# A new hand-written sequence for the operations of a fused attention and swish MLP kernel, and a longer planned transfer for the spread of the reciprocals

## The chip, the cores and the metric

One core of one Trainium2 chip runs the whole kernel. The metric is the device time of one execution in microseconds, lower is better; a time in the tables is the median of several runs. Beside it stands the profile of one execution, whose span runs from the first instruction to the last.

## The reference

Attention over batch 4, 8 heads, 768 positions, head size 64. Three heads (0, 2 and 6) are causal over all positions; the other five are streaming heads, which keep the causal window of 64 positions and the first 4 positions. The result goes through an MLP with a swish whose slope differs per column.

```python
scores = q @ k.T / sqrt(64)
mask   = causal                        for retrieval heads (0, 2, 6)
mask   = causal & (pos_k < 4 | pos_q - pos_k < 64)   for the others
a = softmax(where(mask, scores, -1e9)) ; x = a @ v     # x: 3072 x 512
h = x @ w_in                                           # 512 x 2048
out = (h * sigmoid(beta * h)) @ w_out                  # 2048 x 512, float32
```

## The kernel before

The work is cut into 8 units: unit n = 2b + u is batch b and half u (384 positions, `NQ`). Per unit:

- **Attention.** q, k and v are loaded in float32 on SP's DMA queue, cast to bf16 (tile `c` for q and k, `vb` for v) and turned. Units 0 to 2 turn q and k with TensorE (`T`) and copy the result out (`QK`). From unit 3 on, three loads per tensor fill a `wf` buffer (`load_block`, line 380), GpSimd casts it in six pieces (`cast_block`, line 389), and three DMA transposes on SP write `QK` (`turn_block`, line 397; op `QKb`). Scores `S` go to PSUM, ScalarE takes the exponential (`E`), VectorE multiplies by 0/1 masks (`masks`, line 684, op `M`: a tensor_tensor with both inputs in SBUF). `sums_d` (line 747) adds the columns on TensorE, `pv` (line 840, op `o`) multiplies with v.
- **The window's other operands.** `shift_v` (line 421, op `vs`) copies v shifted by 64 rows, on VectorE or GpSimd; `sink_v` (line 432, op `vk`) makes three small copies on VectorE; `load_edge` and `cast_edge` (`vef`, `ve`) fetch a few rows of v; `kp_copy` (line 556, op `KP`, nine copies) packs keys.
- **The reciprocals, from unit 2 on.** `sums_copy` puts the sums into SBUF, `sums_turn` lays them out by DMA, `recips_d` inverts them, `spread_w` writes them to DRAM (`rd`), and `spread_r` (line 793) reads every row back into 64 partitions (`R`). VectorE's `norm` (line 887, op `xT`) multiplies `o` by `R`. So four steps stand on SP's queue between the sums and `xT`.
- **MLP.** Per unit 16 steps `h` (`mm1`, four matmuls each), ScalarE's tanh (`t`), VectorE's scalar_tensor_tensor (`g`, one SBUF and one PSUM input), and 48 matmuls `m` (`mm2`) in pieces of three; the outputs are copied (`ob`) and stored.
- **Weights.** Eight loads of 1 MB (`wf`,i,0 to 3 for w_in and `wf`,o,0 to 3 for w_out), each cast by GpSimd in four pieces (`wi`,0 to 15 and `wo`,0 to 15). Loads of weights, of v and of the q and k blocks share three `wf` buffers (`RINGS`, line 217): a load is not issued before all casts of an earlier one have run.

**What sets the order.** Every operation is registered with `add` (line 129) with its engine or choice of engines, a planned cost, what it needs and gives, and the buffers that it takes and drops. `_Plan.run` (line 137) goes through the 1096 operations in the order of the list `SEQUENCE` (line 37), takes the engine of each free choice from the string `CHOICE`, gives each a planned start, and the program is written out sorted by it. Each engine's queue, SP's DMA queue too, is then executed strictly in that order: an instruction that waits holds everything behind it on its engine. The planned cost and `dma` of an operation have no other effect than on these starts, and on the number of filling matmuls that keep TensorE busy in unit 0 (`fill`, line 513).

All profile lines carry line 112, the helper that records every operation, so groups are told apart by their tiles. The core of the planner:

```python
e = {"a": "act", "d": "dve", "g": "pool"}[choice[i]] if i in choice else list(costs)[0]
t = max([now[e]] + [done[n][0] - (0.2 if e == "pe" and done[n][1] == e else 0.0) for n in needs])
...
order.append((t, i, f, e, t - was))
...
return [x[2:] for x in sorted(order, key=lambda x: x[:2])]
```

Of the kernel before, what the change touches and what calls it, by code (L numbers as in the profile page):

```python
# [34 lines left out]


SEQUENCE = [
    474, 475, 0, 2, 468, 10, 8, 6, 4, 469, 473, 14, 466, 477, 463, 471, 12, 81, 1, 478, 77, 25, 3, 16, 26, 9,
    33, 11, 479, 20, 35, 34, 5, 27, 18, 36, 28, 7, 29, 42, 31, 30, 13, 53, 480, 32, 82, 15, 50, 41, 37, 51,
    464, 38, 54, 52, 44, 17, 45, 47, 39, 48, 85, 23, 46, 24, 79, 40, 49, 78, 56, 89, 21, 104, 55, 57, 490, 19,  # L40
    43, 58, 59, 22, 100, 60, 61, 101, 482, 62, 83, 476, 80, 91, 73, 63, 90, 485, 102, 74, 75, 484, 64, 103,
    76, 116, 465, 117, 65, 118, 66, 86, 67, 69, 119, 120, 491, 87, 68, 492, 122, 70, 71, 481, 123, 72, 483,
    121, 470, 125, 494, 520, 500, 84, 493, 126, 106, 524, 107, 105, 521, 93, 528, 525, 489, 532, 526, 486, 95,
    128, 127, 529, 112, 92, 88, 522, 97, 536, 530, 113, 495, 114, 537, 108, 115, 109, 124, 129, 538, 503, 540,
    501, 110, 541, 547, 111, 488, 542, 487, 548, 131, 134, 94, 132, 551, 505, 130, 135, 549, 137, 98, 138,
    139, 502, 555, 533, 133, 142, 140, 136, 504, 534, 559, 552, 141, 143, 510, 563, 96, 553, 556, 560, 144,
    99, 467, 561, 496, 155, 557, 499, 564, 145, 497, 157, 498, 156, 506, 515, 523, 146, 507, 570, 509, 527,
    565, 508, 571, 169, 147, 158, 531, 572, 161, 148, 149, 535, 511, 163, 150, 512, 151, 167, 153, 152, 574,
    513, 165, 514, 154, 578, 575, 159, 582, 173, 576, 579, 171, 586, 580, 583, 518, 218, 584, 517, 587, 516,
    588, 519, 592, 596, 593, 539, 597, 168, 543, 546, 170, 544, 550, 164, 598, 222, 188, 160, 554, 594, 189,  # L50
    162, 558, 166, 172, 184, 562, 185, 174, 186, 600, 187, 190, 193, 181, 191, 566, 196, 569, 192, 573, 175,
    194, 604, 220, 567, 198, 605, 219, 577, 601, 201, 221, 581, 199, 197, 585, 602, 225, 589, 200, 228, 608,
    590, 195, 606, 224, 203, 609, 612, 223, 204, 227, 610, 619, 202, 206, 613, 205, 623, 226, 620, 207, 614,
    176, 627, 621, 208, 177, 591, 628, 568, 631, 178, 624, 209, 629, 179, 210, 635, 625, 632, 545, 636, 633,
    229, 237, 637, 642, 239, 646, 238, 235, 650, 182, 643, 240, 647, 644, 595, 241, 211, 648, 654, 212, 242,
    472, 269, 599, 651, 249, 655, 652, 658, 236, 250, 656, 232, 603, 286, 252, 183, 607, 659, 254, 230, 660,
    213, 611, 257, 243, 251, 615, 255, 231, 180, 618, 622, 616, 273, 256, 626, 253, 244, 630, 245, 634, 247,
    246, 638, 258, 248, 641, 639, 645, 287, 233, 259, 617, 214, 260, 216, 215, 261, 649, 272, 653, 217, 271,
    280, 657, 234, 664, 276, 668, 288, 665, 661, 279, 669, 666, 275, 672, 662, 270, 676, 278, 670, 673, 262,
    680, 274, 677, 674, 684, 678, 277, 681, 691, 685, 682, 281, 695, 263, 686, 692, 699, 326, 283, 696, 693,  # L60
    703, 697, 700, 707, 704, 701, 714, 663, 705, 708, 718, 289, 715, 709, 722, 716, 290, 726, 264, 293, 667,
    719, 291, 671, 720, 675, 727, 329, 723, 730, 728, 315, 282, 724, 679, 731, 292, 328, 295, 732, 683, 284,
    298, 687, 296, 690, 294, 694, 319, 297, 300, 688, 698, 301, 285, 702, 303, 299, 265, 302, 304, 267, 327,
    689, 266, 305, 330, 268, 706, 306, 710, 307, 713, 711, 717, 370, 736, 317, 740, 721, 741, 321, 725, 737,
    318, 324, 729, 738, 322, 742, 733, 331, 316, 744, 325, 734, 748, 320, 745, 308, 752, 749, 746, 323, 756,
    750, 753, 763, 757, 754, 309, 767, 366, 758, 764, 771, 768, 765, 775, 769, 772, 779, 712, 773, 332, 786,
    780, 790, 776, 781, 334, 310, 777, 787, 739, 336, 788, 794, 335, 798, 791, 368, 377, 337, 795, 743, 369,
    339, 796, 747, 792, 338, 373, 802, 799, 346, 803, 800, 751, 349, 640, 804, 755, 333, 347, 350, 759, 367,
    762, 760, 341, 371, 766, 344, 340, 770, 374, 372, 342, 774, 345, 348, 351, 375, 778, 343, 354, 782, 376,
    352, 355, 313, 783, 353, 311, 378, 383, 356, 312, 785, 784, 357, 314, 789, 358, 793, 808, 812, 412, 816,  # L70
    813, 387, 817, 814, 797, 390, 386, 801, 388, 820, 818, 359, 392, 389, 821, 360, 805, 809, 416, 822, 395,
    824, 810, 391, 393, 828, 415, 806, 835, 829, 394, 839, 414, 836, 830, 397, 837, 361, 825, 843, 840, 826,
    847, 841, 844, 851, 845, 858, 396, 384, 811, 418, 815, 848, 379, 421, 398, 819, 849, 413, 859, 860, 852,
    862, 807, 853, 866, 863, 399, 870, 400, 419, 864, 867, 823, 871, 422, 874, 872, 364, 401, 417, 868, 875,
    362, 876, 420, 385, 402, 380, 363, 827, 735, 403, 365, 831, 404, 834, 832, 838, 423, 381, 842, 846, 429,
    880, 382, 833, 884, 881, 888, 885, 850, 886, 431, 882, 889, 854, 405, 432, 890, 857, 406, 861, 433, 426,
    865, 425, 855, 869, 424, 856, 430, 761, 873, 427, 434, 436, 892, 407, 877, 435, 896, 878, 893, 900, 897,
    894, 879, 907, 898, 901, 911, 908, 902, 915, 909, 912, 919, 916, 913, 923, 917, 920, 930, 924, 921, 934,
    925, 938, 935, 942, 931, 410, 932, 936, 408, 939, 883, 943, 409, 887, 411, 946, 891, 940, 443, 947, 952,
    446, 948, 895, 944, 444, 956, 953, 960, 954, 899, 445, 961, 447, 438, 962, 903, 439, 437, 906, 964, 441,  # L80
    440, 910, 904, 957, 448, 442, 905, 914, 428, 449, 918, 451, 922, 965, 452, 450, 926, 958, 453, 927, 966,
    929, 928, 454, 933, 455, 968, 972, 969, 979, 970, 937, 980, 983, 981, 941, 984, 945, 973, 985, 987, 974,
    456, 991, 988, 457, 995, 992, 989, 949, 993, 996, 955, 997, 1002, 950, 1006, 1003, 959, 1007, 1004, 458,
    1010, 1008, 1014, 1011, 1018, 1015, 1012, 963, 1016, 1019, 951, 967, 1020, 971, 975, 978, 976, 982, 977,
    986, 990, 994, 998, 1001, 999, 1005, 459, 461, 460, 1009, 462, 1013, 1017, 1021, 1024, 1022, 1028, 1025,
    1023, 1032, 1000, 1029, 1026, 1036, 1030, 1033, 1040, 1037, 1034, 1044, 1038, 1041, 1051, 1045, 1042,
    1055, 1046, 1052, 1059, 1056, 1053, 1063, 1057, 1060, 1067, 1064, 1061, 1073, 1065, 1068, 1076, 1027,
    1077, 1069, 1031, 1074, 1078, 1079, 1075, 1082, 1080, 1085, 1083, 1081, 1035, 1084, 1086, 1039, 1087,
    1043, 1047, 1050, 1048, 1054, 1049, 1058, 1062, 1066, 1070, 1088, 1071, 1089, 1072, 1092, 1090, 1091,
    1093, 1094, 1095,  # L90
]
CHOICE = (
    "dggdaaadgddddaddaddagddaaagaaaggddggddaadaddddaggadaaddggddggaggadddadgaddaaadddaaadaadddddaadaaa"
)


# [21 lines left out]
class _Plan:  # L118
# [10 lines left out]
    def add(self, eng, cost, f, needs=(), gives=(), take=(), drop=(), dma=0.0, mode=None, port=False, begun=()):  # L129

        needs = dict.fromkeys(m for n in needs for m in self.same.get(n, [n]))
        one = isinstance(eng, str)
        alts = [(eng, cost)] if one else list(zip(eng, cost))
        self.ops.append((0, len(self.ops), dict(alts), (lambda e: f()) if one else f, tuple(needs), tuple(gives),
                         tuple(take), tuple(drop), dma, mode, port, tuple(begun)))
# [53 lines left out]
def kernel(  # L189
# [14 lines left out]
    pe, dve, act, pool, sp = (_Ordered(tc, e) for e in (nc.tensor, nc.vector, nc.scalar, nc.gpsimd, nc.sync))  # L204
# [3 lines left out]
    NP = len(PAIRS)  # L208
# [4 lines left out]
    def tpool(name, bufs, space=None):  # L213
# [6 lines left out]
        sp=2, b=4, **{f"es{pi}_{u}": 1 for pi in range(NP) for u in range(2)})  # L220
# [741 lines left out]
    add = plan.add  # L962
    ENG = {"act": act, "dve": dve, "pool": pool, "sp": sp}

    def attention(n, early):
        x = units[n]
        b, u = x.b, x.u

        for pi in range(NP if n < TD else 0):
            for nm in ("q2", "k2"):  # L970
                e = "act" if n == 0 and nm == "k2" else "sp"
                add(e, 0.47, lambda pi=pi, nm=nm, e=e: load_qk(x, pi, nm, ENG[e]), dma=0.63,
                    gives=[("f", n, pi, nm)], take=[(nm + "f", (n, pi), 1)])
# [127 lines left out]
        else:  # L1101
# [3 lines left out]
                take=[("rec", n, 1)], drop=[("sc", n)])  # L1105
            add("dve", 0.35, lambda: recips_d(x), needs=[("sum_t", n)], gives=[("rec", n)])
            add("sp", 0.4, lambda: spread_w(x), needs=[("rec", n)], gives=[("rd", n)], dma=0.1, drop=[("rec", n)])
            add("sp", [1.33, 2.65][u], lambda: spread_r(x), needs=[("rd", n)], gives=[("R", n, t) for t in range(NP)], dma=[4.1, 4.4][u],
                take=[("R", n, 2)] + ([("q2f", (n, "x"), 1)] if u else []))
        for g in range(2):  # L1110
            drop = [(f"es{pi}_{u}", n) for pi in [(0, 1), (2, 3)][g]] + [("vb", b), ("vs", n), ("VE", b)] + ([("KP1", "k")] if n == 1 else [])
# [129 lines left out]
```

The softmax here doesn't subtract the row's maximum and nothing guards it: scores larger than these inputs give would overflow.

## Time and profile before

| | |
|---|---|
| median of 13 runs | 244.98 us (242.68 to 246.46) |
| the profiled execution's own time | 244.87 us |
| its span | 243.2 us |
| time outside the span | 1.67 us |
| TensorE busy | 223.8 us, 92% of the span |
| VectorE, ScalarE, GpSimd busy | 158.4, 137.7, 87.1 us |
| mean granted TensorE clock | 0.993 |
| moved by DMA | 43.14 MB, mean 177 GB/s |
| HBM read, written | 32.38 MB, 6.37 MB |

A group's row gives busy time, mean duration and the idle time of its engine before it, with what ended most of that idle time. A row of the timeline begins with the start in us from the span's start and the duration; "x" is the number of instructions merged; in brackets stands the idle time before it and its releaser. "SPq" is SP's DMA queue. The DMA share of a stretch can exceed 1 where packets of several transfers overlap.

### The profile page before, as it was taken

Reading aid. Unit: us, or ns where it says so; the run is one execution under the profiler, and the core shown is the slowest. Engines: PE = TensorE matmul, PEld = TensorE weight load, DVE = VectorE, ACT = ScalarE, POOL = GpSimd, SP = SyncE. Lnnn points to the kernel's source line nnn. Section 1 sums busy time; section 2 is a strip of 40 time slices with the busy share of each in tenths; the row PEclk is TensorE's granted clock in tenths of the full one; section 3 lists DMA queues with packets and bytes.
Section 4 is the critical chain, followed back from the end, with each engine's and each line's share of the span. In section 5 each row is a group of like instructions: output and inputs, shape, how many; then the busy total and the mean of one; then the engine's idle time right before and its main releaser. Section 6 shows DMA issues by size and latency. Waiting matters only on the chain.

```text
span 243.2 us, 6062 instructions
## 1 busy us (share of the span) xinstructions
PE 223.8 (92%) x2362; PEld 127.9 (53%) x2388; DVE 158.4 (65%) x359; ACT 137.7 (57%) x231; POOL 87.1 (36%) x201
## 2 busy tenths in 40 slices
PE   7795789989979999899999989999999999999994
PEld 6562355545545455446554545564465455465553
DVE  4795599954797869569575457787566847436620
ACT  3656667254859706572379638744674745208611
POOL 6203849497591957263817300624200000000000
PEclk9999799999999999999999999999999999999999
DMA  6999799999978997999999999999620110702012
GB/s 206 254 267 316 234 228 337 310 318 202 189 186 192 213 185 176 170 262 189 233 197 254 210 164 178 211 174 239 199 67 0 46 45 13 214 3 86 0 43 86
DMA packets 92108, 43.14 MB, mean 177 GB/s; under 512 B 75936, under 2 KB 84848, under 8 KB 92080
## 3 DMA queue, kind: packets, MB, share of 16 engines
q1 hardware_dynamic: 90992, 41.98, 75.6%
q10 hardware_dynamic: 1088, 0.79, 1.0%
q8 instruction: 18, 0.29, 0.5%
q14 instruction: 10, 0.08, 0.1%
HBM read 32.38 MB, written 6.37 MB: 159 GB/s over the span
## 4 chain that ended last, share of the span: by engine, by line
PE 63%; DMA 16%; POOL 6%; SPq 5%; issue 4%; DVE 3%; ACT 2%; ACTq 0%; POOLq 0%
PE b L112 55%; PE sp L112 7%; SPq L112 5%; DMA k2f<-in_k_dram 5%; DMA wf<-in_moe_w_in_dram 3%; DMA QK<-c 3%; DMA vf<-in_v_dram 3%; POOL c L112 2%; DMA wf<-in_v_dram 2%; POOL vs L112 1%; DVE gT L112 1%; POOL vb L112 1%; POOL w_in L112 1%; POOL VE L112 1%; ACT t L112 1%
## 5 line engine op out<-in xcount | busy, mean ns | idle before, releaser
L112 ACT ACTIVATE t<-b,beta_h 128x384 f32<-128x384 f32 x128 | 72.2, 582 | 49.0 <-PE b L112 36.5
L112 DVE SCALAR_TENSOR_TENSOR gT<-t,b 128x384 bf16<-128x384 f32 x128 | 68.9, 551 | 40.9 <-ACT t L112 37.4
L112 PE MATMUL b<-xT,w_in 128*128 128x384 bf16 x512 | 92.6, 330 | 2.8 <-DVE mask_s L112 1.1
L112 PE MATMUL b<-w_out,gT 128*128 128x512 bf16 (+1 forms) x374 | 87.6, 370 | 2.5 <-issue 1.6
L112 PEld LDWEIGHTS <-w_in 128*128 128x128 bf16 x512 | 49.3, 99 | 40.1 <-issue 3.6
L112 PEld LDWEIGHTS <-gT 128*128 128x128 bf16 x400 | 37.0, 98 | 38.5 <-issue 2.2
L112 ACT ACTIVATE es<-sp 128x768 bf16<-128x768 f32 (+2 forms) x64 | 48.6, 805 | 11.6 <-PE sp L112 11.4
L112 POOL CAST c<-wf 128x256 bf16<-128x256 f32 x60 | 23.3, 433 | 26.0 <-DMA wf<-in_q_dram 16.2
L112 PE MATMUL sp<-QK 64*64 64x64 bf16 (+6 forms) x402 | 18.8, 234 | 4.5 <-DMA QK<-c 1.7
L112 ACT ACTIVATE osb<-b 128x512 f32<-128x512 f32 (+1 forms) x13 | 7.4, 566 | 22.5 <-PE b L112 18.9
L112 PEld LDWEIGHTS <-QK 64*64 64x64 bf16 (+1 forms) x402 | 10.1, 105 | 15.2 <-issue 11.6
L112 POOL CAST vb<-wf 128x512 bf16<-128x512 f32 x18 | 11.5, 654 | 14.4 <-DMA wf<-in_v_dram 14.4
L112 POOL COPY KP<-QK 128x64 bf16<-128x64 bf16 (+5 forms) x38 | 10.3, 318 | 16.2 <-DMA QK<-c 14.5
L112 DVE TENSOR_TENSOR xT<-sp,R 128x768 bf16<-128x768 f32 (+3 forms) x18 | 11.6, 684 | 7.0 <-PE sp L112 5.8
L112 DVE TENSOR_TENSOR es<-es,mask_c 128x256 bf16<-128x256 bf16 (+2 forms) x32 | 13.4, 427 | 3.2 <-ACT es L112 3.1
L112 POOL CAST w_in<-wf 128x512 bf16<-128x512 f32 x16 | 9.7, 650 | 15.7 <-DMA wf<-in_moe_w_in_dram 15.7
L112 DVE TENSOR_TENSOR es<-es,mask_s 128x800 bf16<-128x800 bf16 (+5 forms) x24 | 13.1, 555 | 2.5 <-ACT es L112 2.5
L112 PE MATMUL sp<-es,vb 128*64 128x64 bf16 (+3 forms) x243 | 13.7, 237 | 0.0
L112 DVE COPY vs<-vb 64x1536 bf16<-64x1536 bf16 (+4 forms) x19 | 11.0, 593 | 3.0 <-POOL vb L112 2.7
L112 PEld LDWEIGHTS <-vb 128*64 128x64 bf16 x243 | 11.5, 111 | 0.5
L112 POOL COPY vs<-vb 64x1536 bf16<-64x1536 bf16 (+2 forms) x7 | 9.6, 1374 | 4.2 <-issue 4.0
L112 POOL CAST w_out<-wf 128x512 bf16<-128x512 f32 x16 | 10.1, 673 | 2.5 <-DMA wf<-in_moe_w_out_dram 2.2
(91 smaller groups left out, 167.5 us busy)
## 6 DMA issues: line engine op xcount, KB each, us to landing
out_dram<-osb SPq DMA_DIRECT2D x23, 256.0 KB
wf<-in_v_dram SPq DMA_DIRECT2D x18, 256.0 KB
wf<-in_moe_w_out_dram SPq DMA_DIRECT2D x4, 1024.0 KB
wf<-in_q_dram SPq DMA_DIRECT2D x15, 256.0 KB
wf<-in_k_dram SPq DMA_DIRECT2D x15, 256.0 KB
R<-rd SPq DMA_DIRECT2D x9, 384.0 KB
wf<-in_moe_w_in_dram SPq DMA_DIRECT2D x4, 768.0 KB
q2f<-in_q_dram SPq DMA_DIRECT2D x12, 192.0 KB
```

Of the source, the lines that this page charges most:

```text
L112: ins = f(*a, **k)
```

## The change

Three things are edited: the list `SEQUENCE`, the string `CHOICE` and two planned durations.

```diff
 SEQUENCE = [
-    474, 475, 0, 2, 468, 10, 8, 6, 4, 469, 473, 14, 466, 477, 463, 471, 12, 81, 1, 478, 77, 25, 3, 16, 26, 9,
...
+    474, 475, 6, 466, 4, 8, 14, 468, 12, 478, 467, 20, 10, 0, 2, 16, 5, 469, 473, 9, 7, 33, 471, 29, 77, 34,
...
 CHOICE = (
-    "dggdaaadgddddaddaddagddaaagaaaggddggddaadaddddaggadaaddggddggaggadddadgaddaaadddaaadaadddddaadaaa"
+    "aaddagaggdgdadadadaadddaddaaddgaagggdaaadaadaaaddaaaddaggdgdgaggadggdgdaadaadaaadaadadadadddadaaa"
 )
...
-            add("sp", [1.33, 2.65][u], lambda: spread_r(x), ..., dma=[4.1, 4.4][u],
+            add("sp", [1.33, 2.65][u], lambda: spread_r(x), ..., dma=[6.2, 6.0][u],
```

No operation is added or removed and no tile changes; TensorE's program has three filling matmuls fewer (4771 rows against 4777, a weight load and a matmul each). What moves on the queues, as the two programs stand:

```
SP queue (f = q/k load, vf = v load, wf = weights, vef = edge rows, st = store, numbers are units)
before, start: f0 q x3, beta, f0 q, f1 q x2, vf0 x3, wf i0, f1 x3, wf i1, f1 x2, wf o0, f1, | wf i2, vf1 x3, wf o1, wf o2, wf i3, wf o3, f2 x8
after,  start: f0 q x3, vf0, f0 q, vf0, f1 q x2, vf0, f1 x2, wf i1, f1, vf1, wf i0, beta, wf o0, f1 x3, | wf i2, vf1 x2, wf o1, wf o2, f2, wf i3, wf o3, f2 x7
before, later: vef1, vf2, QKb3 x3, st, st, sums2, st, vf3, vef1, rd2, f4 q, vef2, R2, f4 k, vef2, st, sums3, vf4, QKb4 x3, rd3, vf5, st, R3
after,  later: vf2, vef1, vef1, QKb3 x3, st, sums2, vf3, st, rd2, f4 q, R2, f4 k, st, sums3, vf4, QKb4 x3, rd3, vf5, st, R3
before, later: f5 q, f5 k, st, sums4, f6 k, QKb5 x3, rd4, f6 q, st, R4, vf6, st, QKb6 x3
after,  later: f5 q, f5 k, st, st, sums4, f6 k, QKb5 x3, st, rd4, f6 q, vef2, vef2, R4, QKb6 x3, vf6

GpSimd: wi casts before: 1, 3, 4, 5, 0, 2, 7, 6;  after: 5, 6, 4, 0, 3, 1, 2 ... 7
engine changes from unit 2 on (45 in all, the rest in units 0 and 1 or single copies of ob, sums, QK):
  vs 2 GpSimd -> VectorE; vs 4 and vs 7 VectorE -> GpSimd; KP 6 VectorE -> GpSimd; KP 7 GpSimd -> VectorE
  ve 1 and ve 2 GpSimd -> VectorE; ve 3 VectorE -> GpSimd
TensorE: first h step of unit 0 stands ahead of the last 11 S and T steps of unit 1 in the order before, ahead of the last 6 in the order after
  the first S of unit 4 stands 2 steps later; o of units 3 and 4 stand one m step later
VectorE: vk 2 to 5 stand later; by the planned starts vk 3, 4 and 5 fall beside GpSimd's KP 4, 5 and 6
ScalarE: its four loads of unit 0's k stood together; now the first Exp stands after two of them
```

## Prediction

> **What bounds the kernel.** I read the page first, then TensorE in stretches of 25 us, then its waits, then what ended them.
>
> ```profile
> span 243.2 us, 6062 instructions
> PE 223.8 (92%) x2362; PEld 127.9 (53%) x2388; DVE 158.4 (65%) x359; ACT 137.7 (57%) x231; POOL 87.1 (36%) x201
> ```
>
> TensorE is 92% busy and every other engine has room. The change leaves all its useful matmuls in place, so it can only win or lose TensorE's idle time and its time at half clock. Where that lies, in the columns start:end, length, busy time of PE, PEld, DVE, ACT, POOL, granted clock, DMA share, GB/s:
>
> ```profile
> 0.00:25.00 25.00, 17.94 (x263) 13.41 (x267) 17.34 (x61) 14.29 (x23) 8.11 (x36) 1.00 0.96 264
> 25.00:50.00 25.00, 21.67 (x258) 12.60 (x259) 20.40 (x43) 13.74 (x25) 16.42 (x28) 0.93 0.98 278
> 50.00:75.00 25.00, 23.42 (x235) 12.87 (x238) 15.96 (x35) 16.91 (x29) 19.08 (x41) 1.00 0.97 216
> 75.00:100.00 25.00, 24.14 (x270) 13.05 (x271) 20.50 (x42) 15.48 (x27) 13.97 (x23) 1.00 0.95 189
> 100.00:125.00 25.00, 23.49 (x263) 13.17 (x265) 17.27 (x38) 12.34 (x22) 12.13 (x27) 1.00 1.03 219
> 125.00:150.00 25.00, 23.91 (x326) 12.82 (x329) 13.60 (x36) 17.95 (x29) 7.65 (x22) 1.00 1.07 196
> 150.00:200.00 50.00, 49.42 (x492) 27.21 (x498) 34.49 (x72) 29.82 (x52) 9.75 (x26) 1.00 0.59 128
> ```
>
> Idle: 7.1 us before 25, 3.3 to 50, then 1.6, 0.9, 1.5 and 1.1 per 25 us, and 0.6 in the 50 us after 150. Three regimes, then. Up to about 49 us the kernel waits for data: DMA is full, and the last quarter of w_in ends that stage. From 50 to 150 a few single waits stand in a full TensorE. After 150 nothing is left to win. The single waits, from TensorE's timeline:
>
> ```profile
> 49.30 1.48 PE L112 MATMUL b<-xT,w_in 128*128 128x384 bf16 x8 [1.03 <-POOL w_in L112]
> ...
> 70.29 0.68 PE L112 MATMUL b<-es,one 128*32 128x384 bf16 x19 [1.31 <-DVE gT L112]
> ...
> 87.09 1.09 PE L112 MATMUL b<-es,one 128*32 128x384 bf16 x25 [0.44 <-DVE es L112]
> ...
> 102.37 0.50 PE L112 MATMUL sp<-QK 64*128 64x384 bf16 x6 [1.15 <-DMA QK<-c]
> ...
> 145.06 0.50 PE L112 MATMUL sp<-QK 64*128 64x384 bf16 x6 [0.51 <-DMA QK<-c]
> ```
>
> The sums of units 2 and 3 wait for masks (the bracket at 70.29 names gT; the last mask ends at 69.77 and is what the sums need). The first scores of units 4 and 6 wait for DMA transposes. What held the masks, on VectorE:
>
> ```profile
> 68.23 1.54 DVE L112 TENSOR_TENSOR es<-es,mask_c 128x256 bf16<-128x256 bf16 x1
> ...
> 82.48 1.54 DVE L112 COPY vs<-vb 4x896 bf16<-4x896 bf16 x1
> 84.05 1.54 DVE L112 COPY vb<-vb 4x512 bf16<-4x512 bf16 x2
> ```
>
> The same shapes later, with GpSimd idle, take 0.27 us (mask, at 113.03) and 0.39 + 0.39 us (vk 4, at 111.42). On GpSimd stand, in those two moments, vs 2 (three copies, 68.02 to 71.27) and vs 3 (two, 81.88 to 85.35).
>
> **The change part by part.**
>
> *Start, value -0.5 us, from -1.3 to +1.5.* Before, GpSimd is idle 11.93 to 18.32 for w_in's first quarter and then does w_in's second quarter ahead of the rest of the first, so the first buffer is free at 26.88; SP issues nothing from 19.91 to 26.90, and DMA falls to a share of 0.51 in 26.2 to 29.6. New: quarter 1 is loaded first, then one v load, then quarter 0. Ahead of the later of the two, which was cast from 24.59 on, the queue now holds one v load more (1.45 us: by the trace's packets unit 0's three took 8.0 to 12.4) and one f load less (0.6 us): it lands near 24.6 + 0.9 = 25.5, four casts of 0.56 free its buffer at 27.8, and the queue's packets end at 26.4 + 1.4 = 27.8, so of 1.8 us of empty DMA some 0.8 goes. w_in's last quarter landed at 48.5 and its first h step ran at 49.30; another 0.5 us of gaps near 39 to 42 close as well (wf o1 and o2 no longer wait behind v), one f load of 0.6 us goes ahead: 48.5 - 0.8 - 0.5 + 0.6 = 47.8. But TensorE must have come that far. Its first h step waits for xT of unit 0, which stands later now: about 27.3 for 26.4; five fewer S and T steps follow it (about 1.6 us), and the 1.80 us wait for a k load at 19.93 is gone, since that load now stands ahead of the weights. It then waits about 1.3 us for wi 8, cast behind v. I put it at 48.7, 0.6 earlier, and take 0.5. New waits: ScalarE's cast of the f1 q load behind wf o0 holds three Exps, and TensorE's T behind it; landing late by 1 us would cost that. At half clock TensorE spent 3.4 us (26.2 to 29.6); it still waited 1.03 us afterwards, so I count nothing for it, either way up to 1.7 us, inside the range.
>
> *Sums of unit 2, -1.0 (from -1.3 to 0).* vs 2 leaves GpSimd for VectorE, at a place after the masks. VectorE pays 1.2 us (vs 6 took 1.19), under TensorE's h and m steps. The mask falls from 1.54 to 0.27. I keep 0.3 for GpSimd's q and k casts beside the masks.
>
> *Sums of unit 3, -0.6 (from -0.8 to 0).* From first to last sum 86.30 to 87.94 = 1.64 us; unit 5's identical 28 take 0.88: 0.76 of delay. vs 3 moves behind the six casts of unit 4, so vk 2 costs 0.8 for 3.1. I keep 0.15.
>
> *First scores of unit 4, -1.1 (from -1.2 to 0).* SP's edge loads of unit 2 (1.38 and 1.18 us of issue) and a store move behind. SP was waiting for itself: sums 2 at 71.63, then the v load, edge rows and stores up to 77.10, while the reciprocal was ready at 75.93; f4 k landed at 92.4. New: sums 2 at about 70.6, reciprocal about 74.6, f4 k about 90.7; GpSimd casts it at once instead of after ve 2 (1.1 us), so the transposes issue from about 92.3 instead of 95.16 and end near 96.5 for 100.48. TensorE asks for them 1.3 us later in its own order.
>
> *First scores of unit 6, -0.5 (from -0.5 to 0).* The v load of unit 6 (SP busy 129.90 to 135.50) and a store wait (1.27) no longer stand ahead of its transposes; R4 and two edge loads do.
>
> *The spread.* Longer planned numbers change no instruction. R2's packets ran 82.78 to 88.49, and xT of unit 2 waited 0.98 us for them at 89.77 while TensorE had m steps. New: R2 issues about 3 us earlier and `o` of unit 2 stands 2 us later against its sums. Worth 0.
>
> *What it adds, +0.8 (from 0 to +5.2).* vs 4 (and vs 7) and KP 6 go to GpSimd; vk 3, 4 and 5 fall beside KP groups (nine copies, 2.48 us at 126.97). "SBUF — State Buffer" (Who interferes with whom) says that VectorE copies, and tensor_tensor with two SBUF inputs, share a port with GpSimd, and that the later one waits until the other's instruction ends. By the row of vk 2 beside vs 3 each vk would lose 2.3 us; by the rule a KP copy holds it only for its 0.28 us, three times 0.28 = 0.8. The nearest row is vk 5 beside GpSimd's 0.35 us casts: 0.62 + 0.78 = 1.40, against vk 3's 1.29. So I take the rule's 0.8 at most, under m steps, plus one mask of unit 4 beside vs 4 that is partly seen: 0.8 in all.
>
> Sum: -0.5 - 1.0 - 0.6 - 1.1 - 0.5 + 0.8 = -2.9. Span 243.2 - 2.9 = 240.3; the 1.67 us outside stay: 241.97. The profiled execution (244.87) lies 0.11 under the median, so 242.1; I say 242.0.
>
> **Rivals.**
>
> *The gains are given back at unit 5.* GpSimd began KP 5 at 126.97 as the transposes landed, TensorE its scores at 126.91: no slack. If DMA and not SP's waits sets that landing, an earlier TensorE only waits there, and all up to then shrinks to the edge rows' 0.7 us; with unit 6's 0.5: 244.98 - 1.2 = 243.8. For it: DMA's share is about 1. Against it: SP's own waits fell out above, 70 to 75 and 90 to 95 have a share near 0.63.
>
> *The port holds for whole groups (slower).* If a vk waits out its KP group, 2.3 us each; of that a run of h steps hides about 1 us (four banks): vk 3 and 4 cost 1.3 each, vs 4 beside unit 4's masks costs 1.3 as vs 2 did, KP 6 on GpSimd 2.48 instead of 1.14 us delays unit 6's next scores by 1.3: 5.2 for my 0.8, so 242.0 + 4.4 = 246.4. It decides from the point where a vk takes over 1.8 us. For it: the rows of vk 2. Against it: vk 5.
>
> *Nothing real changes:* the planned times are not the chip's; waits only change place: 245.0.
>
> **How the numbers follow.** Main case 0.55 (own range 239.8 to 243.4); full gains without new costs, 240.6, lie inside it. Given back at unit 5 0.20 (243.1 to 244.6); slower 0.15; nothing changes 0.10. What a measurement can tell from no change is about 0.5%: 243.75 to 246.2. Faster: main nearly whole, 0.55, and half of unit 5's, 0.10. Slower: 0.15, and 0.02 of the rest. Same 0.18. The range, 239.8 to 245.6, leaves out the slower case and a little on either side.
>
> **What would show it.** Right: the sums of units 2 and 3 without brackets, vk 2 at 0.8 us, the first scores of units 4, 5 and 6 without a DMA wait, w_in's last quarter used at 48 to 49. Wrong: a second stretch at half clock before 50, the first h step after 29, vk 3 or 4 over 1.8 us, or a wait for QK at unit 5.

## The result, and the profile after

| | before | the change |
|---|---|---|
| median of all runs | 244.89 us (48 runs, 241.99 to 247.79) | 241.55 us (11 runs, 240.57 to 242.64) |
| ratio to before | | 0.9888, 95% from 0.9863 to 0.9913 |
| the profiled execution's own time | 244.87 us | 243.23 us |
| its span | 243.2 us | 241.5 us |
| mean granted TensorE clock | 0.993 | 0.986 |

The change is 3.3 us faster where 2.9 us was forecast. Medians below are of all executions, while the ratios leave out those more than 1.5% above the fastest of their kernel (15 of before's 29 beside e5 to e8, and the profiled ones of e5, 244.70 us, and e6, 452 us: e6's profile is not read, and e5's only where another profile shows the same kind of thing).

The execution that was profiled is a late one: 243.23 us lies above all eleven timed runs. So I read it beside a second profile of the same instruction order (experiment e1, own time 241.01 us, planned duration put back). First the engines' busy times from the page of the changed kernel:

```profile
PE 223.6 (93%) x2359; PEld 128.5 (53%) x2385; DVE 152.3 (63%) x354; ACT 141.8 (59%) x238; POOL 88.4 (37%) x199
```

TensorE's busy time is the same as before (223.6 for 223.8 us): what changed is where it stands still. The stretches of the changed kernel, with the columns of before (length, busy time of PE, PEld, DVE, ACT, POOL, granted clock, DMA share, GB/s):

```profile
0.00:25.00 25.00, 18.57 (x253) 14.27 (x254) 13.94 (x54) 16.25 (x28) 7.35 (x33) 0.86 0.96 263
25.00:50.00 25.00, 20.33 (x257) 11.93 (x257) 18.57 (x37) 14.83 (x25) 15.96 (x26) 1.00 0.92 266
50.00:75.00 25.00, 24.55 (x241) 13.20 (x242) 17.30 (x49) 17.52 (x30) 16.35 (x39) 1.00 0.98 216
75.00:100.00 25.00, 24.42 (x273) 13.57 (x276) 18.48 (x41) 16.34 (x27) 10.86 (x19) 1.00 1.12 204
100.00:125.00 25.00, 24.63 (x270) 13.68 (x270) 16.16 (x32) 13.85 (x25) 16.18 (x32) 1.00 1.11 221
125.00:150.00 25.00, 23.63 (x333) 12.68 (x341) 15.51 (x34) 18.36 (x30) 11.87 (x35) 1.00 1.04 210
```

Idle from 50 to 125 us is 0.45 + 0.58 + 0.37 = 1.4 us, where before had 1.6 + 0.9 + 1.5 = 4.0. From 125 to 150 there is more of it (1.37 for 1.09); 25 to 50 has 4.7 us for 3.3, and 0 to 25 has 6.4 for 7.1. The single places, in TensorE's timeline of the changed kernel; a row without a bracket had no wait:

```profile
50.72 4.19 PE L112 MATMUL b<-xT,w_in 128*128 128x384 bf16 x24 [0.34 <-POOL w_in L112]
...
69.02 0.69 PE L112 MATMUL b<-es,one 128*32 128x384 bf16 x19
...
85.65 1.11 PE L112 MATMUL b<-es,one 128*32 128x384 bf16 x28
...
101.76 0.50 PE L112 MATMUL sp<-QK 64*128 64x384 bf16 x6
...
125.88 0.50 PE L112 MATMUL sp<-QK 64*128 64x384 bf16 x4 [0.79 <-DMA QK<-c]
...
142.15 0.50 PE L112 MATMUL sp<-QK 64*128 64x384 bf16 x6
```

These are the rows of the prediction one by one: the sums of units 2 and 3 and the first scores of units 4 and 6 have lost their brackets; w_in's last quarter is used later, not earlier; and unit 5 has a wait for transposes that before did not have.

To put sizes to this I cut the run at TensorE steps that have the same set of TensorE steps ahead of them in both orders, and take the distance between their starts (for the first four cuts and the last, the start of the matmul just ahead of the step). "m to 15" is the piece of three m matmuls that ends with the fifteenth:

| stage, up to the start of | before | change | e1 | forecast | change - before | e1 - before |
|---|---|---|---|---|---|---|
| weights: m to 15 of unit 0, right behind the h steps on w_in's last quarter | 53.18 | 54.59 | 52.62 | -0.5 | +1.41 | -0.56 |
| sums of unit 2: h step 10 of unit 1 | 18.23 | 16.85 | 16.85 | -1.0 | -1.38 | -1.38 |
| sums of unit 3: h step 2 of unit 2 | 21.64 | 20.96 | 20.96 | -0.6 | -0.68 | -0.68 |
| first scores of unit 4: m to 12 of unit 2 | 12.85 | 11.58 | 11.59 | -1.1 | -1.27 | -1.26 |
| unit 5: the third scores of unit 5 | 25.98 | 26.87 | 26.61 | 0 (and +0.8 for all that is added) | +0.89 | +0.63 |
| first scores of unit 6: h step 8 of unit 4 | 20.09 | 19.47 | 19.47 | -0.5 | -0.62 | -0.62 |
| rest, to the last step | 86.93 | 86.94 | 86.94 | 0 | +0.01 | +0.01 |
| sum | 238.90 | 237.26 | 235.04 | -2.9 | -1.64 | -3.86 |

These two executions of one order agree to 0.01 us in five of the six stages after the first, and differ by 0.26 at unit 5. The weights stage differs by 1.97 us. One profile cannot tell what the new start is worth; the next runs could.

### The profile page after: what moved, and what is told of

Same layout as the page of the kernel before. It is cut to its first block, busy times and chain, and to the rows that moved or that the text cites. A ratio compares the mean times of both kernels' runs of the same rounds, so it can differ in the third digit from the quotient of the medians.

```text
span 241.5 us, 6057 instructions
## 1 busy us (share of the span) xinstructions
PE 223.6 (93%) x2359; PEld 128.5 (53%) x2385; DVE 152.3 (63%) x354; ACT 141.8 (59%) x238; POOL 88.4 (37%) x199
## 4 chain that ended last, share of the span: by engine, by line
PE 68%; DMA 15%; POOL 6%; SPq 5%; issue 4%; ACT 1%; DVE 1%; POOLq 0%
PE b L112 60%; DMA wf<-in_moe_w_in_dram 9%; PE sp L112 8%; SPq L112 5%; DMA q2f<-in_q_dram 3%; POOL w_in L112 2%; POOL c L112 2%; DMA QK<-c 1%; DMA k2f<-in_k_dram 1%; POOL vb L112 1%; POOL vs L112 1%; ACT es L112 1%; DVE es L112 1%; ACT c L112 0%; ACT osb L112 0%
## 5 line engine op out<-in xcount | busy, mean ns | idle before, releaser
L112 PE MATMUL b<-xT,w_in 128*128 128x384 bf16 x512 | 90.1, 326 | 2.3 <-DVE beta_h L112 1.1
L112 ACT ACTIVATE es<-sp 128x768 bf16<-128x768 f32 (+3 forms) x64 | 49.1, 807 | 11.4 <-PE sp L112 11.1
L112 ACT ACTIVATE osb<-b 128x512 f32<-128x512 f32 (+1 forms) x14 | 8.0, 568 | 23.5 <-PE b L112 17.0
L112 POOL COPY KP<-QK 128x64 bf16<-128x64 bf16 (+4 forms) x36 | 10.0, 327 | 21.6 <-DMA QK<-c 15.6
L112 DVE TENSOR_TENSOR es<-es,mask_c 128x256 bf16<-128x256 bf16 (+2 forms) x32 | 12.6, 407 | 5.0 <-ACT es L112 4.8
L112 PE MATMUL sp<-es,vb 128*64 128x64 bf16 (+3 forms) x243 | 14.9, 245 | 0.0
L112 DVE TENSOR_TENSOR es<-es,mask_s 128x800 bf16<-128x800 bf16 (+5 forms) x24 | 12.0, 513 | 2.5 <-ACT es L112 2.4
L112 DVE TENSOR_SCALAR osb<-b 128x512 f32<-128x512 f32 x11 | 7.5, 681 | 9.5 <-PE b L112 7.9
L112 POOL COPY vs<-vb 64x1536 bf16<-64x1536 bf16 (+2 forms) x9 | 12.2, 1359 | 3.2 <-issue 2.9
L112 PEld LDWEIGHTS <-vb 128*64 128x64 bf16 x243 | 12.5, 116 | 0.5
```

The source lines that it names most:

```text
L112: ins = f(*a, **k)
```

## The experiments

Every kernel was timed beside before, so before's own median differs from run to run. Numbers in the diffs are operation numbers in the list `SEQUENCE`. I tested theory A, the sums of the prediction read stage by stage, against a rival for each stage.

**e1, the planned number alone**

```diff
-spread_r ... dma=[6.2, 6.0][u]
+spread_r ... dma=[4.1, 4.4][u]
```

> The changed kernel with the spread's planned duration put back to 4.1 and 4.4 us, sequence and choices as in the change. My theory: on each engine the instructions stand in the same order, so this is the changed kernel again: 241.5 us, ratio to before about 0.986 to 0.989. Rival: the new number is what makes the new order work, then the gain of 3.3 us goes wholly or in part: 243 to 245 us. It is also a second look at the changed kernel: if the start's loss is a property of the order and not of one execution, the first h step on w_in's last quarter stands again near 50.7 us (49.3 before).

Measured: 241.26 us against 244.50 for before, ratio 0.9862 (0.9822 to 0.9903). The planned number is worth nothing that these runs can tell. TensorE at the end of the weights stage (PEld is the load of the weights for those matmuls), and at unit 5:

```profile
48.75 3.54 PE L112 MATMUL b<-xT,w_in 128*128 128x384 bf16 x20 [0.71 <-DVE xT L112]
48.75 0.44 PEld L112 LDWEIGHTS <-w_in 128*128 128x128 bf16 x4 [1.20 <-POOL w_in L112]
...
116.42 7.31 PE L112 MATMUL b<-xT,w_in 128*128 128x384 bf16 x44 [0.47 <-ACT osb L112]
```

Here w_in's last quarter is used at 48.75 us (the prediction said 48.7). The matmul's bracket names VectorE's `xT`, but the last `xT` of unit 1 had ended at 48.28; GpSimd's cast of the quarter's first piece ended at 48.70, and the weight load names it. So TensorE still waited for the weights, as in the change (cast to 50.67, used at 50.72). The last row shows another form of the loss at unit 5: TensorE waits for ScalarE's copy of an output block.

**e2 and e3, the two halves exchanged**

```diff
-SEQUENCE = the change's list
+e2: before's list for the operations up to 539 (the last m that waits for weights), the change's list for the rest
+e3: the change's list up to 539, before's list for the rest
```

> Order and engine choices of before for all operations up to the last m step of unit 0 that waits for the weights (about 55 us), the changed kernel's for the rest. Theory A (the start lost 1.4 us, all else is gained later): w_in's last quarter is used at 49.3 us again, and the time falls by 1.4 us against the changed kernel, to 240.1 us. Rival B (the later lag in the start is one execution's, or is taken up by a later wait): 241.5 us as the change. Rival C (the new start is what brings the gain): over 243 us.

> The converse: the changed kernel's order and choices up to about 55 us, before's for the rest. Theory A: the start alone costs 1.4 us, of which the wait of 0.5 us for the first scores of unit 4 can hide a part: 245.8 to 246.3 us. Rival B: 244.9 us, as before. Rival C: under 244 us.

Measured: e2 242.30 us, ratio 0.9929 (0.9889 to 0.9969); e3 245.59 us, ratio 1.0015 (0.9981 to 1.0048; its median is 1.1 us above before's). Theory A falls for the start: with before's start the kernel gets no better, but 0.8 to 1.0 us worse by the medians than the change and e1. Eight executions with the change's start are profiled (the change, e1, e3, e5, e7, e8, e10, e11): they end the weights stage at 54.59, 52.62, 52.41, 54.40, 51.34, 51.33, 51.58 and 51.35 us, mean 52.45. Three with before's start (before, e2, e9) end it at 53.18, 53.44 and 53.72, mean 53.45. So the new start gains about 1 us. The scatter of 3.3 us and only three profiles of the other start leave that size rough, but e2's time agrees with it, and the +1.41 of the profiled execution was one draw.

e3 shows that the new start alone is no gain. Its sums of unit 2 wait longer than those of before. TensorE and VectorE of e3:

```profile
70.63 0.68 PE L112 MATMUL b<-es,one 128*32 128x384 bf16 x19 [2.43 <-DVE gT L112]
```

```profile
66.14 1.80 DVE L112 TENSOR_TENSOR es<-es,mask_s 128x800 bf16<-128x800 bf16 x1
67.87 1.05 DVE L112 TENSOR_TENSOR es<-es,mask_c 128x128 bf16<-128x128 bf16 x1
68.85 0.78 DVE L112 TENSOR_TENSOR es<-es,mask_s 128x400 bf16<-128x400 bf16 x1
```

GpSimd's three copies of vs 2 run from 66.06 to 69.41 us in e3 and cover the last masks of unit 2 nearly whole (the first of these rows takes 0.57 us in e1; the first copy ends at 67.52, this mask at 67.95). TensorE comes 0.8 us earlier and the sums start at 70.63 instead of 70.29: what came from the start, and more, is lost at the next stage (19.34 us for 18.23).

**e4, the v load behind w_in's quarter 0**

```diff
-SP: ..., 91, 97 (vf 1), 480 (wf i0), 485, ...
+SP: ..., 91, 480 (wf i0), 97 (vf 1), 485, ...
```

> The changed kernel with one edit: the load of a third of batch 1's v, which stands on SP's queue ahead of w_in's quarter 0, is put behind it. Theory A (the weights stage is late because that load of 0.5 MB goes ahead of the second quarter): quarter 0 lands 1.4 us earlier, its casts end near 27.2 instead of 28.6 us, w_in's last quarter is used at 49.3 instead of 50.7 us, and the time is 240.1 to 240.5 us. Rival: the load takes its 1.4 us wherever it stands before the last quarter, so that only the gap in DMA near 26 to 29 us shrinks and the last quarter is used later than 50.2 us: 241.2 to 241.5 us.

Measured: 240.90 us, ratio 0.9838 (0.9800 to 0.9877). Quarter 0's casts end at 25.93 us, against 26.9 to 28.6 in the eight executions with the change's start, and the first cast of the last quarter starts at 45.47, against 46.8 to 50.1. That part of theory A holds. The time does not follow in full: in this execution the last quarter was used at 48.92, 2.8 us after its first cast had ended, and TensorE's row there has no bracket. TensorE itself was late; its clock was 0.80 from 20 to 25 us and 0.75 from 40 to 45. The profile of e5, with the change's start, also has half clock that late (41.1 to 44.5 us) and used the quarter 2.9 us after its cast. So behind the weights stands TensorE as a second limit of the stage, and where it lies depends on the execution. e12 below makes the same move and has no half clock after 21.7 us: it used the quarter at 46.90, right after the cast (46.81) and before every other profile here. The gain in time of 0.4 us against e1 is within what these runs can tell.

**e5 and e6, vs 2 on GpSimd or on VectorE**

```diff
 e5, from the change:
-VectorE: ..., 652, 179 (vs 2), 236, ...
+GpSimd: ..., 177, 178 (last v cast), 179 (vs 2), 235 (KP 3), ...
 e6, from before:
-GpSimd: ..., 178, 179 (vs 2), 235, ...
+VectorE: ..., 652, 179 (vs 2), 236, ...
```

> The changed kernel with the shift of v for unit 2 put back on GpSimd, right behind the v casts and so beside unit 2's masks. Theory A (VectorE's mask copies and GpSimd's copies hold each other up): one mask of unit 2 takes about 1.5 us again, the sums of unit 2 wait 1 us or more, and the time rises by 1.0 to 1.5 us to 242.5 to 243.0 us. Rival (the sums came earlier because of the order of TensorE's own steps, and the copy has nothing to do with it): masks at 0.3 to 0.7 us, time 241.5 us.

> The kernel before with one edit: the shift of v for unit 2 goes to VectorE behind unit 2's masks. Theory A: the sums of unit 2 lose their wait (0.7 us in a bracket, 1.0 to 1.5 us by the progress of TensorE), but SP's edge loads still stand ahead of unit 4's transposes, so that part of it can be given back there: 243.5 to 244.3 us. Rival (a single move does nothing without the rest of the order): 244.9 us.

Measured: e5 243.09 us, ratio 0.9921 (0.9879 to 0.9963), by the medians 1.5 us above the change; e6 243.07 us, ratio 0.9919 (0.9868 to 0.9969), by the medians 1.6 us below its before (244.71). Each is about theory A's forecast, e6 a little better than it; for e6 only the time says so. With this one copy back, the stage of unit 2's sums takes 18.82 us for 16.85. In e5 GpSimd makes the three copies of vs 2 from 64.83 to 68.37 us and the nine of KP 3 from 69.66 to 72.47. The first two copies of vs 2 and VectorE's masks:

```profile
64.83 1.46 POOL L112 COPY vs<-vb 64x1536 bf16<-64x1536 bf16 x1
66.33 1.14 POOL L112 COPY vs<-vb 64x1024 bf16<-64x1024 bf16 x1
...
65.27 1.30 DVE L112 TENSOR_TENSOR es<-es,mask_c 128x512 bf16<-128x512 bf16 x1
66.49 1.40 DVE L112 TENSOR_TENSOR es<-es,mask_s 128x800 bf16<-128x800 bf16 x1
...
69.85 0.50 DVE L112 TENSOR_TENSOR es<-es,mask_c 128x128 bf16<-128x128 bf16 x1
```

The same in the changed kernel, with no vs 2 on GpSimd:

```profile
64.31 0.41 DVE L112 TENSOR_TENSOR es<-es,mask_c 128x512 bf16<-128x512 bf16 x1
65.23 0.73 DVE L112 TENSOR_TENSOR es<-es,mask_s 128x800 bf16<-128x800 bf16 x1 [0.51 <-ACT es L112]
...
67.99 0.22 DVE L112 TENSOR_TENSOR es<-es,mask_c 128x128 bf16<-128x128 bf16 x1
```

The first two masks take 0.89 and 0.67 us longer, and each ends 0.3 to 0.4 us after the GpSimd copy that was running when it began (66.57 behind 66.29, 67.89 behind 67.47). Beside the first KP copy (69.66 to 70.27) the last one takes 0.28 us longer and ends at 70.35. The kernel before shows the same: its mask from 68.23 to 69.77 stands beside the first copy of vs 2, which ends at 69.63:

```profile
68.02 1.61 POOL L112 COPY vs<-vb 64x1536 bf16<-64x1536 bf16 x1
```

**e7, the edge loads put back**

```diff
-SP: ..., f4 q, 213 (R2), 273 (f4 k), ..., 366 (f6 q), 286, 287 (vef 2, both), 310, ...
+SP: ..., f4 q, 286 (vef 2), 213 (R2), 273 (f4 k), 287 (vef 2), ..., 366 (f6 q), 310, ...
```

> The changed kernel with the two edge loads of unit 2 put back on SP's queue, one ahead of the spread of the reciprocals and one behind the k load of unit 4, as before. Theory A (they held up unit 4's transposes by their issue of 2.5 us): the transposes issue about 2.5 us later, TensorE waits for QK at the first scores of unit 4 again, about 1 us, and the time rises to 242.3 to 242.7 us. Rival (the transposes came earlier because the sums and reciprocals of units 2 and 3 came earlier): no wait over 0.3 us, 241.5 us.

Measured: median 243.05 us against 244.71 for before, so 1.5 to 1.8 us above the change and e1. The ratio, 0.9985 (0.9937 to 1.0032), counts 14 of before's 29 runs and hardly shows it; compared with the 17 runs of the change and e1 themselves, e7's mean is 1.5 us higher (95% from 0.7 to 2.2, by resampling). The size is a little above theory A's, but the place is not. TensorE of e7:

```profile
98.83 0.50 PE L112 MATMUL sp<-QK 64*128 64x384 bf16 x6
...
116.74 6.74 PE L112 MATMUL b<-xT,w_in 128*128 128x384 bf16 x40 [1.09 <-ACT osb L112]
124.10 0.50 PE L112 MATMUL sp<-QK 64*128 64x384 bf16 x4 [0.61 <-DMA QK<-c]
```

The first scores of unit 4 have no wait with the edge loads back, and their stage takes 11.58 us as in the change. The loads make unit 4's transposes about 0.7 us later against TensorE (last issue 6.28 us after h step 2 of unit 2, 5.58 in e1), and that fits into slack. What rises in this profile is unit 5 (28.00 us for 26.61) and the rest (88.52 for 86.94). It is not shown that the edge loads did that: unit 5 takes 27.4 us in e2 and e4 too, and the rest 88.6 and 88.8 in e10 and e11, all with the edge loads where the change has them. That the edge loads cost 1.5 us is measured; where they cost it stays open.

**e8, unit 5's transposes freed**

```diff
-GpSimd: ..., 329, 330 (vs 5), 317, 321, 316, 318, 320, 322 (casts of unit 5), 332, ...
+GpSimd: ..., 329, 317, 321, 316, 318, 320, 322, 330 (vs 5), 332, ...
-SP: ..., 307, 370 (f6 k), 324, 323, 325 (QKb 5), ...
+SP: ..., 307, 324, 323, 325 (QKb 5), 370 (f6 k), ...
```

> The changed kernel with two moves for unit 5: on GpSimd the shift of v for unit 5, which waits for TensorE's o of unit 3, goes behind the six casts of unit 5's q and k; on SP the k load of unit 6 goes behind the three transposes of unit 5. Theory A (unit 5's first scores wait 0.8 us for transposes that stood behind these two): the transposes issue from about 116.5 instead of 118.8 us, the wait goes, and the time falls by 0.8 to 1.0 us to 240.5 to 240.7 us. Rival (given back again): the k load of unit 6 is late for unit 6's transposes, and the wait only moves to unit 6: 241.5 us.

Measured: 241.27 us, ratio 0.9883 (0.9828 to 0.9937): no gain. In the changed kernel GpSimd stands still ahead of vs 5, which needs the buffer that TensorE's o of unit 3 reads until 112.0 us, with the casts of unit 5 behind it:

```profile
112.10 2.97 POOL L112 COPY vs<-vb 64x1536 bf16<-64x1536 bf16 x2 [2.86 <-issue]
115.13 4.18 POOL L112 CAST c<-wf 128x256 bf16<-128x256 f32 x12
```

In e8 the casts and the transposes come earlier, unit 5 takes 26.20 us without a wait, and unit 6 takes 20.89 for 19.47. TensorE there:

```profile
139.75 0.50 PE L112 MATMUL sp<-QK 64*128 64x384 bf16 x6 [0.68 <-DMA QK<-c]
```

The rival holds: what unit 5 gained is given back at unit 6. It is not only that this execution was early: e10 and e11 come to unit 6 as early, have that k load where the change has it, and do not wait there.

**e9, only TensorE's two steps**

```diff
-TensorE: ..., 722, 290 (first S of unit 4), 726 (h), 667 (m), 671, ...
+TensorE: ..., 722, 726 (h), 667 (m), 290 (first S of unit 4), 671, ...
```

> The kernel before with one edit: on TensorE the first scores of unit 4 stand behind one more h step and one m step, as in the change; SP's queue and GpSimd's stay word for word. Theory A (that wait of 1.15 us went in the change because TensorE asks two steps, 1.3 us, later; moving the edge loads was not needed): no wait for QK over 0.3 us at the first scores of unit 4, TensorE is 1.1 us ahead there; what is left at the end depends on unit 5, where before had no slack, so 243.6 us if it is kept and 244.7 us if it is given back. Theory B (SP's edge loads made the wait): 1 us of wait stays and TensorE is no further than before.

Measured: 244.81 us against 244.25 for before, ratio 0.9993 (0.9952 to 1.0034). TensorE of e9:

```profile
103.33 0.50 PE L112 MATMUL sp<-QK 64*128 64x384 bf16 x6
...
105.79 0.81 PE L112 MATMUL b<-xT,w_in 128*128 128x384 bf16 x4 [0.56 <-DVE gT L112]
```

The wait of 1.15 us for the transposes is gone with SP's queue and GpSimd's untouched, so theory B falls: the edge loads did not have to move for it. But half of it comes back two steps later as a wait for `gT`: the stage takes 12.36 us, between before's 12.85 and the change's 11.58, and nothing is left at the end.

**e10, e11 and e12, trying for a better version**

```diff
 e10, from the change:
-SP: ..., 326 (vf 5), 264 (R3), ..., 689, 545 (store of block 0 of unit 0), 307, ...
+SP: ..., 326 (vf 5), 545 (store), 264 (R3), ..., 689, 307, ...
 e11 = e10 and, on GpSimd, 330 (vs 5) behind 322
 e12 = e11 and, on SP, 97 (vf 1) behind 480 (wf i0)
```

> The changed kernel with one edit: the store of unit 0's first output block, which before issued at 72 us and in the change at 114 us, goes behind the v load of unit 5 (about 100 us), where SP waits anyway. Theory A (the store holds one of three output buffers, so ScalarE's copy of a block of unit 2 waits for it and TensorE behind it): the copy of that block no longer stands behind the store, no wait for the output copy near 117 us, and 0 to 0.5 us less than the change, 240.9 to 241.4 us. Rival (the copy waits for something else on ScalarE): a wait of about 0.5 to 1.1 us near 117 us stays.

> The store moved as in the run before, and the shift of v for unit 5 moved on GpSimd behind unit 5's six casts; the k load of unit 6 stays where the change has it. Theory A (unit 5 gives back through these two, and the loss at unit 6 came from the late k load): neither a wait for the output copy near 117 us, nor for QK at units 5 and 6; 240.7 us. Rival (DMA itself sets when unit 5's operands land): a wait for QK of 0.5 us or more at unit 5 stays, 241.4 us.

> The three moves together: store early, shift of v behind unit 5's casts, and the load of a third of batch 1's v behind w_in's quarter 0. Theory A: 240.2 to 240.7 us, the best of all. Rival (TensorE, not DMA, ends the weights stage once quarter 0 is earlier): no better than the run before it, 240.7 to 241.2 us.

Measured: e10 241.41 us, ratio 0.9879 (0.9828 to 0.9929); e11 241.61 us, 0.9912 (0.9877 to 0.9948); e12 240.31 us, 0.9844 (0.9793 to 0.9895). What ended the wait of ScalarE's output copy is told by its own row. In e1, then in e11, with TensorE behind it:

```profile
115.77 0.60 ACT L112 ACTIVATE osb<-b 128x512 f32<-128x512 f32 x1 [1.15 <-DMA out_dram<-osb]
```

```profile
164.60 0.60 ACT L112 ACTIVATE osb<-b 128x512 f32<-128x512 f32 x1 [8.22 <-DMA out_dram<-osb]
...
165.25 0.81 PE L112 MATMUL b<-xT,w_in 128*128 128x384 bf16 x4 [1.12 <-ACT osb L112]
```

It waits for a store to land. There are three output buffers, and while unit 0's block waits for its store it holds one of them. The bracket is all of ScalarE's idle time and not what the store cost: in e12 the same copy stands behind 6.84 us of idle time that TensorE ended. The cost is TensorE's bracket, 1.12 us in e11.

With the store where the change has it, ScalarE stands idle 1.1 to 2.4 us ahead of its copy of unit 2's block, until a store lands, in all seven profiles (the change, e1, e2, e4, e5, e7, e8), and TensorE waits behind it 0.5 to 1.1 us in four (e1, e2, e4, e7). With the store moved (e10, e11, e12) that copy of ScalarE's does not wait for a store; in e10 it runs at 113.73 us. So moving the store does what theory A says, but the time shows no gain from it alone: e10's execution was 2.8 us further ahead than the change's at that place, and a copy of unit 4's block then waited for another late store. The stage to the end took 88.6 and 88.8 us in e10 and e11 for 86.94. In e11 a wait for QK of 0.42 us at unit 5 stayed as well, as its rival said. e12 has none of these waits, a rest of 87.55 us and the best median, about 1 us under the change; but its interval overlaps the change's, and why its stores landed in time and those of e11 did not was not tried.

One more place takes back what an early start gains. TensorE of e12 at the first scores of unit 3:

```profile
69.25 0.50 PE L112 MATMUL sp<-QK 64*128 64x384 bf16 x4 [0.66 <-DMA QK<-c]
```

e12 ends the weights stage at 50.76 us, 1.9 us before e1, and waits here. e7, e8, e10 and e11, which end it at 51.3 to 51.6, wait 0.22 to 0.52 us here; e1 and the change do not. So the stage of unit 3's sums repeats to 0.01 us only while TensorE arrives late enough: e12 takes 21.65 us for it, as before did.

## Why the prediction was right, and where it was not

The time was forecast at 242.0 us and is 241.55. The main gains came where they were placed; two further terms came out in size by luck, with a cause that was not theirs. Step by step:

- **Start, -0.5.** About -1.0 by the mean of eight executions against three, well inside the bounds given (-1.3 to +1.5), which is what the scatter needed. One term of its working was miscounted: ahead of the later quarter both orders have nine f loads, not one fewer; only the v load is added. So quarter 0's casts end at 26.9 to 28.6 us (27.8 was said with the miscount), and in e4, with that v load behind it, they end 1 us or more earlier. The wait that was named (TensorE behind ScalarE's cast of a q load) was there: 1.71 us in the profiled execution, 0.70 in e1. Another was left out: the change puts the load of beta behind quarter 0, and TensorE waits 1.12 us (0.67 in e1) for it.
- **Sums of unit 2, -1.0.** -1.38. That the copy vs 2 holds the masks is right (e5 by its trace, e6 by its time). The step from the mask to the sums was misread (below), which may be the 0.4 us that was missing. The 0.3 kept for GpSimd's casts does show in masks (0.73 and 0.69 us beside v casts, 0.57 and 0.29 for the same shapes later), but not in those that the sums wait for.
- **Sums of unit 3, -0.6.** -0.68. vk 2's copies take 0.47 and 0.39 us where they took 1.54 each. It was not isolated by a run of its own.
- **First scores of unit 4, -1.1.** -1.27, but the step failed in its cause. The prediction led with the edge loads on SP and named TensorE's own 1.3 us beside them, without asking whether one would do. With the edge loads back (e7) the stage is as short, and with TensorE's order alone (e9) the wait goes as well. The edge loads are worth 0.7 us there, not 2.5; the transposes' issue ends at 97.64 us, 2.8 earlier than before where 4.0 was forecast. The slack is there twice: TensorE asks 1.3 us later, and GpSimd no longer stops for the 1.1 us of ve 2 between the casts of unit 4. How much of the 1.27 us belongs to the second of these was not tried.
- **First scores of unit 6, -0.5.** -0.62. That the v load and the store made the wait was not isolated. e8 shows the slack that the gain stands on: with the k load of unit 6 behind unit 5's transposes (issued from 118.98 us, for 113.78 in e1) the wait is back.
- **The spread's number, 0.** Right (e1).
- **What it adds, +0.8.** The size is right by luck, and the cause is wrong. The port that VectorE and GpSimd share cost TensorE no wait there that before does not have: vk 3 beside a KP group took 1.61 us for 1.29, vk 5 1.44 for 1.40, and one mask of unit 4 beside vs 4 1.23 for 0.27, all under TensorE's other steps. The loss stands at unit 5 (0.9 us in the change, 0.6 in e1, 1.4 in e2 and e4). In the change it is a wait for transposes, which the prediction itself named as a sign of being wrong; in e1, e2 and e4 a wait for an output buffer. The prediction counted the store that moves behind as a gain on SP's queue and did not ask what the store holds: it was issued at 72 us before and at 114 in the change, and kept one of three output buffers for that time.
- **Rivals.** "Given back at unit 5" (0.20) was right in mechanism and too large: the place had no slack and took back 0.6 to 1.4 us, not all. "The port holds for whole groups" is wrong: no vk took over 1.8 us. That "nothing real changes" is wrong by the time (ratio 0.9888, 95% up to 0.9913) and by e5.

What the sums of unit 2 waited for in before is the bracket's `gT` after all. They start at 70.29, not behind the last mask (to 69.77) but behind VectorE's next instruction, to 70.24:

```profile
69.70 0.54 DVE L112 SCALAR_TENSOR_TENSOR gT<-t,b 128x384 bf16<-128x384 f32 x1
```

By the program, this `gT` frees the PSUM bank (the buffer for matmul results) that the sums write. It stands behind the masks, so the late mask made it late too. In the change the sums take a bank that an earlier `gT` frees, and they start at 69.02, after the last mask (to 68.69) and without a wait. No run isolated how much of the 1.38 us that is worth.

The rule of the Trainium skill on which the 0.8 was built, in "SBUF — State Buffer" (Who interferes with whom), that the later engine waits until the other's instruction ends, fits these traces: in e5, e3 and before the masks end 0.1 to 0.4 us after the GpSimd copy that was running when they began. It would also explain why a mask loses 0.28 us beside the short copies of KP 3 and up to 1.3 beside a long one of vs 2. The rule fits; I used it where TensorE had cover, and the price came from elsewhere.

## What to carry to other kernels

- When a transfer is moved back on a queue, ask what its source buffer keeps occupied in the meantime. The store cost nothing where it left and made a wait 40 us later.
- One profile does not price a stage that ends with DMA: the same start ended its weights stage up to 3.3 us apart, while the later stages of two executions mostly repeated to 0.01 us. Cut the run at common steps, and take the noisy stage from several executions.
- A removed wait is a gain only if the next place has slack. Undo one edit in the new kernel as well as doing it alone in the old one: e5 and e6 agreed, but for the edge loads the place I had priced showed no wait, and the time went up by 1.5 us all the same.
- A bracket names what came last by the profile, and it can be one of several. Check it against the ends of all that the step needs, the buffer it writes included: the sums waited for a bank and not for a mask, and e1 for a weight and not for `xT`.

## What the runs showed of the hardware

TensorE's stretch at half clock moved from 26.2 to 29.6 us (before) to 18.1 to 24.9 us in the change's profile, where it is twice as long, and in e1 nearly none is left (clock 0.999). The mean clock says little about the time: of the 18 executions of this order in the change's and e1's runs, seven with a clock of 0.993 or more have a mean of 241.1 us and eleven below it 241.8. Where the stretch lies may count for more: only e4 and e5 have one between 39 and 45 us, and they are the ones in which TensorE came 2.8 and 2.9 us after the weights (0.84 in e3, whose stretch ends at 25.6; under 0.1 in the other profiles with this start). An output store of 256 KB whose issue ended at 160.8 us in e11 released its buffer only at about 164.6: a landing of 3.8 us in a stretch with other loads on the queue.
